# The start of a fused convolution and feed-forward kernel on one core: softmax, bands, masks and exchanges arranged differently

## The chip, the cores and the metric

The kernel runs on one core of a Trainium2 chip. The core has TensorE (matrix products, called PE in the profile, its weight loads PEld), VectorE (DVE), ScalarE (ACT), GpSimd (POOL) and SyncE (SP). Each takes its own instructions in order, and they wait for each other by semaphores. The metric is the device time of one execution in microseconds (us). Times in the text are us from the start of the profiled span.

## The reference

What is computed is a lightweight convolution followed by a multiplicative feed-forward layer.

```python
# x: (8, 3904, 192), weight: (8 heads, 7 taps)
w = softmax(weight, axis=-1)
out[b, s, h*24:(h+1)*24] = sum over k of w[h, k] * x_padded[b, s + k, h*24:(h+1)*24]   # 6 zero rows ahead
t = out.reshape(31232, 192)
a = t @ w1          # 192 x 1024
b = t @ w2          # 192 x 1024
h = (a * b) @ w3    # 1024 x 1024
result = h @ w_out  # 1024 x 192, float32
```

Since nothing stands between `w3` and `w_out`, the kernel multiplies these two with each other once (`W_sb`) and then uses their product.

## The kernel before, in words

The tokens are cut into two halves (`NS = 2`), which are worked side by side: half r sits on partitions 64r to 64r + 63, so that two products with 64 rows each run in TensorE at once. The convolution works on windows of 64 rows, of which 58 are new tokens. For each head it is a product with a band matrix, `Aband`, that holds the seven softmax weights on seven diagonals. The windows go in blocks; their number in each block stands in `SIZES` (line 50), and there are 270 in all.

**The prologue** (lines 132 to 213). ScalarE's queue loads the 8 x 7 weights into all 128 partitions (line 133), and GpSimd's queue loads x for block 0 (lines 98 and 129). GpSimd then makes `cmask`, seven diagonals of 64 x 64 (line 148), and starts the loads of `w1` and `w2`, with the identity for transposes between their halves (lines 159 to 166). TensorE meanwhile multiplies zeros 16 times (`warm`, lines 169 to 174). VectorE and ScalarE compute the softmax in every partition (lines 180 to 188). `band(g, copies)` (line 201) makes the bands of four heads: a product of masks and weights (`cprod`, line 203), three adds (line 211), and two copies that exchange the partition halves (line 213). It is called once per half of the heads; the first half's convolution stands between.

**The first block.** `conv(b, h0, nh)` (line 229) does 16 products for four heads into one PSUM tile, `cps`, and copies it into `convo` in pieces (line 255). `pe_transposes(b)` (line 287) turns `convo` by TensorE and copies the result into three tiles `xT` (line 300): the first and third on VectorE, the second on ScalarE. `swap_w(k, half, engines)` (line 315) makes `wsw`, a copy of the weights `wn` with the partition halves exchanged, 64 x 512 at a time (line 318). There are twelve such copies, six for each half of the columns.

**The rounds.** `first_product(R)` (line 326) does 512 tokens of each half. For each of eight column tiles ft, twelve products fill two PSUM tiles `pa` and `pb` (line 339); ScalarE copies `pa` into `asb` (line 345), and VectorE multiplies it with `pb` into `abT` (line 346). PSUM has four such tiles (`banks`), given out in turn, and conv, transposes, `warm` and the rounds all draw on them. `second_product` (line 351) multiplies `abT` with `W_sb`. The order of all work is written out by hand: a dictionary names what follows each ft in rounds 0 to 2 (conv of the next blocks, their transposes, and `fold`, which makes `W_sb`). From round 3 on, `xT` is filled by DMA transposes from `rows` in HBM.

**The queues.** GpSimd issues all loads of x, `w1`, `w2`, `w3` and `w_out` in program order between its own instructions, and after eight of them waits for an older one to land before it issues the next. The main part calls, in this order: load x of blocks 1 and 2, band, conv, band, three more `warm`, an exchange, conv, transposes, the other exchanges, and the later loads (lines 404 to 424).

Of the kernel before, what the change touches and what calls it, by code (L numbers as in the profile page):

```python
# [8 lines left out]

FP32 = mybir.dt.float32  # L10
# [7 lines left out]
def kernel(  # L18
# [53 lines left out]
    def slot(shape, dtype, name):  # L72
        return stage.tile(shape, dtype, tag="slot", bufs=5, name=name)
# [55 lines left out]
            nc.gpsimd.dma_start(out=xb[Q * r + PAD:Q * r + Q, 0, :],  # L129
                                in_=x_rows[r * TS:r * TS + ST, :])  # L130
# [8 lines left out]
    zeros = const.tile([128, CH], BF16)  # L139
    nc.vector.memset(zeros, 0.0)  # L140
    nc.scalar.activation(out=tiny, in_=tiny, func=ACT.Exp)

    ones = const.tile([128, 1], BF16)
    nc.gpsimd.memset(ones, 1.0)
    cmask = const.tile([128, K, Q], BF16)
    for r in range(NS):
        ps = slice(Q * r, Q * r + Q)
        nc.gpsimd.affine_select(
            out=cmask[ps], in_=ones[ps].unsqueeze(2).to_broadcast([Q, K, Q]),
            pattern=[[-1, K], [-1, Q]], compare_op=ALU.is_equal,  # L150
            fill=0.0, base=0, channel_multiplier=1)
    wn = [const.tile([128, DFF], BF16, name=f"wn{k}", tag=f"wn{k}") for k in range(3)]
    wsw = [const.tile([128, DFF], BF16, name=f"ws{k}", tag=f"ws{k}") for k in range(3)]

# [7 lines left out]
        nc.gpsimd.dma_start(out=wn[1][:, cs], in_=moe_w2[0:128, cs])  # L162

    load_w(0)
    ident = const.tile([128, 128], BF16)
    make_identity(nc, ident)
    load_w(1)

    def warm(n):
        t = banks("warm")  # L170
        for j in range(n):
            nc.tensor.matmul(t[:, j % 2, :], zeros[:, 0:128], zeros, start=True, stop=True)  # L172

    warm(16)


    wmax = const.tile([128, H], FP32)
    wsum = const.tile([128, H], FP32)
    wsb = const.tile([128, 2, 2, K], BF16)
    nc.vector.reduce_max(out=wmax, in_=wall, axis=AX.X)  # L180
    nc.vector.tensor_tensor(
        out=wall, in0=wall, in1=wmax.unsqueeze(2).to_broadcast([128, H, K]), op=ALU.subtract)
    nc.scalar.activation(out=wall, in_=wall, func=ACT.Exp)
    nc.vector.reduce_sum(out=wsum, in_=wall, axis=AX.X)
    nc.vector.reciprocal(out=wsum, in_=wsum)
    for r in range(NS):
        ps = slice(Q * r, Q * r + Q)
        nc.vector.tensor_tensor(
            out=wsb[ps],
            in0=wall[ps].rearrange("p (g a e) k -> p g a e k", g=2, a=2)[:, :, r],  # L190
            in1=wsum[ps].rearrange("p (g a e) -> p g a e", g=2, a=2)[:, :, r].unsqueeze(3)
                .to_broadcast([Q, 2, 2, K]),
            op=ALU.mult)

    Aband = const.tile([128, 2, 2, 2, Q], BF16)

# [1 line left out]
        g, j, e = h // 4, (h % 4) // 2, h % 2  # L198
        return Aband[Q * r:Q * r + Q, g, int(j != r), e, :]

    def band(g, copies):
        c = slot([128, 2, K, Q], BF16, "cprod")
        nc.vector.tensor_tensor(  # L203
            out=c,
            in0=cmask.unsqueeze(1).to_broadcast([128, 2, K, Q]),
            in1=wsb[:, g].unsqueeze(3).to_broadcast([128, 2, K, Q]),
            op=ALU.mult)
        for out, i0, i1 in ((c[:, :, 0:3], c[:, :, 0:3], c[:, :, 4:7]),
                            (c[:, :, 0:2], c[:, :, 0:2], c[:, :, 2:4]),
                            (Aband[:, g, 0], c[:, :, 0], c[:, :, 1])):  # L210
            nc.vector.tensor_tensor(out=out, in0=i0, in1=i1, op=ALU.add)  # L211
        for f, d, e in zip(copies, (Q, 0), (0, Q)):
            f(out=Aband[d:d + Q, g, 1], in_=Aband[e:e + Q, g, 0])


    xT = [const.tile([128, RING], BF16, name=f"xT{k}", tag=f"xT{k}") for k in range(NP)]
# [12 lines left out]
    def conv(b, h0, nh, evict=None):  # L229
        n = SIZES[b] // 2  # L230
        if h0 == 0:
            convo_of[b] = work.tile([128, n, NP, NS, Q], BF16, tag="convo", bufs=2, name="convo")
        convo = convo_of[b]
        cps = banks("cps")
        wd = nh * G

        def view(ps, r):
            return cps[ps, r, 0:n * wd].rearrange("p (w g) -> p w g", g=wd)

        for j in range(nh):  # L240
            h = h0 + j
            for c in range(2):
                xb, w0 = xb_of[b][c]
                for r in range(NS):
                    nc.tensor.matmul(  # L245
                        view(slice(Q * c, Q * c + Q), r)[:, :, j * G:(j + 1) * G],
                        band_of(h, r),
                        xb[Q * r:Q * r + Q, w0:w0 + n, h * G:(h + 1) * G],
                        start=True, stop=True)
        src = cps[:, :, 0:n * wd].rearrange("p r (w g) -> p r w g", g=wd)  # L250
        o = 0
        for e, (k, c0, m) in enumerate(segments(h0 * G, wd)):
            dst = convo[:, :, k, :, c0:c0 + m].rearrange("p w r g -> p r w g")
            f = evict or [nc.scalar.copy]
            f[e % len(f)](out=dst, in_=src[:, :, :, o:o + m])  # L255
            o += m
        if h0 + nh == H:
            del xb_of[b]
# [25 lines left out]
                    nc.sync.dma_start(out=dst[s0:s1], in_=src[s0:s1])  # L284
                w += m

    def pe_transposes(b):
        n = SIZES[b] // 2
        convo = convo_of[b]
        tps = banks_bf16("tps")  # L290
        for k in range(NP):
            for w in range(n):
                nc.tensor.transpose(
                    out=tps[:, k * n + w, :],
                    in_=convo[:, w, k].rearrange("p r g -> p (r g)"), identity=ident)
        t0 = tok(FIRST[b])
        for k in range(NP):
            dst = xT[k][:, t0:t0 + 2 * n * ST].rearrange("p (c w s) -> p c w s", c=2, w=n)
            src = tps[:, k * n:(k + 1) * n, :].rearrange("p w (c s) -> p c w s", c=2)
            (nc.scalar.copy if k == 1 else nc.vector.tensor_copy)(out=dst, in_=src[:, :, :, 0:ST])  # L300

    def transposes(R, first=0):
        t0, t1 = max(R * CH, first), min((R + 1) * CH, TS)
# [73 lines left out]
    def load_wo():  # L377
        nc.gpsimd.dma_start(out=wo_b, in_=wor)
# [34 lines left out]
    swap_w(2, 0, (V, A))  # L413
    swap_w(1, 0, (V, A))
    for k in (0, 2, 1):
        swap_w(k, 1, (P, A))
    load_wo()
    for jt in range(4):
        load_w3(jt)
    load_x(3)  # L420
    for jt in range(4, JT):
        load_w3(jt)
    for b in (4, 5, 6):
        load_x(b)

    def seq(*fs):
        def run():
            for f, *a in fs:
                f(*a)
        return run  # L430

    def fold(jt):
        if jt < JT:
            w3_transpose(jt)
        if jt > 0:
            w3_product(jt - 1)

    first_product(0, {
        2: seq((conv, 1, 0, 4)),
        4: seq((conv, 1, 4, 4)),  # L440
        6: seq((pe_transposes, 1)),
        7: seq((conv, 2, 0, 4))})
    first_product(1, {
# [90 lines left out]
```

## Time and profile before

| | us |
|---|---|
| median of the runs shown | 537.17 |
| lowest and highest of the three | 536.29 and 537.28 |
| the profiled execution's own time | 537.5 |
| its span, first to last instruction | 535.4 |
| TensorE busy within the span | 524.8 |
| VectorE busy | 349.7 |
| ScalarE busy | 326.3 |
| GpSimd busy | 49.1 |

The span is what the profile covers; the profiled execution's own time is longer by what lies around it. A TensorE that is busy is not one at its peak, since its products are pipelined and their ends are modelled. A row of a timeline has the start, the length, the engine, the line, the operation, the tile written and the tiles read, their sizes, and in brackets how long the engine had been idle and what ended that.

### The profile page before, as it was taken

How to read it: one execution, taken by the hardware profiler on the slowest of the kernel's cores; microseconds unless marked ns; L12 is line 12 of the kernel's file. 1: busy time of each engine (PE TensorE's matmuls, PEld its weight loads, DVE VectorE, ACT ScalarE, POOL GpSimd, SP SyncE). 2: the span in 40 equal slices, each digit the busy share in tenths (PEclk: the TensorE clock that was granted, in tenths of full speed). 3: DMA queues.
4: the chain of work that ended last, by engine and by line, in shares of the span. 5: the costliest groups of instructions: out<-in, count | busy, mean ns of one | idle time of the engine just before them, and what ended most of it. 6: DMA issues, size and time to landing. Idle time of an engine off the chain costs nothing.

```text
span 535.4 us, 12799 instructions
## 1 busy us (share of the span) xinstructions
PE 524.8 (98%) x5504; PEld 346.7 (65%) x5504; DVE 349.7 (65%) x329; ACT 326.3 (61%) x373; POOL 49.1 (9%) x87
## 2 busy tenths in 40 slices
PE   7999999999999999999999999999999999999996
PEld 2455584765858567585675857658576684856676
DVE  5577729669395784948849397593966929377470
ACT  3866647557474665747647475573756747475562
POOL 8641001001010010200101000020000000000000
PEclk9899999999999999999999999999999999999999
DMA  8999466766389555995569736593307443130304
GB/s 100 184 203 192 76 149 146 121 177 74 124 154 148 121 67 144 135 145 118 68 164 146 145 88 97 148 143 116 77 31 187 83 133 78 61 103 12 110 1 149
DMA packets 130587, 63.13 MB, mean 118 GB/s; under 512 B 83398, under 2 KB 129506, under 8 KB 130530
## 3 DMA queue, kind: packets, MB, share of 16 engines
q1 hardware_dynamic: 91842, 45.65, 36.4%
q0 software_dynamic: 38544, 16.63, 26.7%
q8 instruction: 43, 0.70, 0.6%
q14 instruction: 14, 0.11, 0.1%
q10 hardware_dynamic: 144, 0.03, 0.0%
HBM read 33.28 MB, written 34.82 MB: 127 GB/s over the span
## 4 chain that ended last, share of the span: by engine, by line
PE 92%; DVE 3%; ACT 2%; DMA 1%; issue 1%; ACTq 0%; DVEq 0%
PE ops L357 31%; PE pa L339 29%; PE pb L339 28%; PE cps L245 3%; DVE abT L346 2%; ACT asb L345 1%; PE wps L397 1%; PE w3ps L388 1%; DMA wall<-in_weight_dram 1%; ACT ws L318 1%; DVE cprod L203 0%; DVE cprod L211 0%; DVE xT L300 0%; ACT convo L255 0%; ACT xT L300 0%
## 5 line engine op out<-in xcount | busy, mean ns | idle before, releaser
L346 DVE TENSOR_TENSOR abT<-asb,pb 128x1024 bf16<-128x1024 bf16 (+1 forms) x248 | 298.1, 1204 | 56.3 <-ACT asb L345 41.0
L345 ACT CAST asb<-pa 128x1024 bf16<-128x1024 f32 (+1 forms) x248 | 247.6, 999 | 69.8 <-PE pa L339 69.0
L339 PE MATMUL pb<-xT,wn 64*128 64x512 bf16 (+1 forms) x744 | 202.2, 373 | 0.4
L339 PE MATMUL pa<-xT,wn 64*128 64x512 bf16 (+1 forms) x744 | 199.1, 374 | 1.7 <-DVE xT L300 1.1
L339 PE MATMUL pa<-xT,ws 64*128 64x512 bf16 (+1 forms) x744 | 199.2, 374 | 0.1
L339 PE MATMUL pb<-xT,ws 64*128 64x512 bf16 (+1 forms) x744 | 194.6, 374 | 0.0
L339 PEld LDWEIGHTS <-wn 64*128 64x128 bf16 x1488 | 137.8, 94 | 81.1 <-issue 5.6
L339 PEld LDWEIGHTS <-ws 64*128 64x128 bf16 x1488 | 128.3, 94 | 70.9 <-issue 5.6
L357 PE MATMUL ops<-W_sb,abT 128*128 128x192 bf16 x1952 | 166.3, 246 | 0.0
L357 PEld LDWEIGHTS <-abT 128*128 128x128 bf16 x1952 | 159.6, 98 | 9.9 <-issue 9.5
L362 ACT COPY osb<-ops 128x768 f32<-128x768 f32 (+1 forms) x62 | 48.9, 788 | 117.0 <-PE ops L357 117.0
L255 DVE CAST convo<-cps 128x864 bf16<-128x864 f32 (+10 forms) x46 | 37.9, 858 | 104.3 <-PE cps L245 101.2
L108 POOL DMA_DIRECT2D xb<-in_x_dram x36 | 28.6, 804 | 13.6 <-PE pa L339 4.6
L487 POOL COPY pace<-abT 1x2 bf16<-1x2 bf16 x9 | 1.6, 174 | 270.3 <-DVE abT L346 270.3
L255 ACT CAST convo<-cps 128x640 bf16<-128x640 f32 (+9 forms) x40 | 22.6, 607 | 1.1 <-PE cps L245 0.6
L245 PE MATMUL cps<-xb,Aband 64*64 64x432 bf16 (+3 forms) x384 | 18.8, 285 | 1.9 <-DVE Aband L211 1.4
L245 PEld LDWEIGHTS <-Aband 64*64 64x64 bf16 x384 | 7.1, 105 | 10.8 <-issue 7.7
L172 PE MATMUL warm<-zeros 128*128 128x512 bf16 x19 | 7.3, 559 | 1.4 <-DVE zeros L140 1.4
L397 PE MATMUL wps<-wo_b,w3T 128*128 128x192 bf16 x64 | 6.6, 246 | 0.4 <-DVE xT L300 0.4
L399 ACT CAST W_sb<-wps 128x192 bf16<-128x192 f32 x8 | 2.5, 319 | 5.9 <-PE wps L397 5.9
L388 PEld LDWEIGHTS <-w3b 128*128 128x128 bf16 x64 | 3.7, 98 | 3.4 <-issue 3.4
L172 PEld LDWEIGHTS <-zeros 128*128 128x128 bf16 x19 | 2.4, 135 | 5.4 <-issue 3.8
(46 smaller groups left out, 58.9 us busy)
## 6 DMA issues: line engine op xcount, KB each, us to landing
out_dram<-osb SPq DMA_DIRECT2D x60, 384.0 KB
xb<-in_x_dram POOLq DMA_DIRECT2D x18, 432.0 KB, 7.0
rows<-convo SPq DMA_DIRECT2D x8, 648.0 KB
w3b<-in_moe_w_dram POOLq DMA_DIRECT2D x8, 256.0 KB, 10.9
xb<-in_x_dram POOLq DMA_DIRECT2D x4, 384.0 KB, 12.4
xb<-in_x_dram POOLq DMA_DIRECT2D x4, 336.0 KB, 10.0
xT<-rows SPq DMA_TRANSPOSE x84
rows<-convo SPq DMA_DIRECT2D x4, 288.0 KB
```

Of the source, the lines that this page charges most:

```text
L108: nc.gpsimd.dma_start(out=xb[Q * r:Q * r + Q, w:w + m, :], in_=x_spans(r, i, m))
L172: nc.tensor.matmul(t[:, j % 2, :], zeros[:, 0:128], zeros, start=True, stop=True)
L245: nc.tensor.matmul(view(slice(Q * c, Q * c + Q), r)[:, :, j * G:(j + 1) * G], band_of(h, r), xb[Q * r:Q * r + Q, w0:w0 + n, h * G:(h + 1) ...
L255: f[e % len(f)](out=dst, in_=src[:, :, :, o:o + m])
L318: f(out=wsw[k][d:d + Q, cs], in_=wn[k][e:e + Q, cs])
L339: nc.tensor.matmul(p[:, r, 0:N], w_of(i, k, r)[rs, ft * 128:(ft + 1) * 128], xT[k][rs, r0:r0 + N], start=(k == 0), stop=(k == NP - 1))
L345: nc.scalar.copy(out=asb[:, :, 0:N], in_=pa[:, :, 0:N])
L346: nc.vector.tensor_tensor(out=ab[:, ft, :, 0:N], in0=asb[:, :, 0:N], in1=pb[:, :, 0:N], op=ALU.mult)
L357: nc.tensor.matmul(ops[:, g // 2, (g % 2) * D:(g % 2) * D + D], ab[:, jt, r, g * 128:(g + 1) * 128], W_sb[:, jt, :], start=(jt == 0), stop ...
L362: nc.scalar.copy(out=osb.rearrange("p (a g) d -> p a (g d)", g=2), in_=ops[:, 0:ng // 2, 0:2 * D])
L388: nc.tensor.transpose(out=tps[:, gt, :], in_=w3b[:, gt * 128:(gt + 1) * 128], identity=ident)
L397: nc.tensor.matmul(wps[:, 0, 0:D], w3T[:, gt, :], wo_b[:, gt, :], start=(gt == 0), stop=(gt == JT - 1))
```

## The change

- **Softmax.** The weights are loaded once, with a head per partition (8 x 7). The sum comes with the exponential, as its accumulated output. A product with a diagonal puts the weights of head h into row h alone, and one matmul with ones spreads them over 128 partitions into PSUM. Two copies on VectorE bring them into `wsb`, each weight twice side by side.
- **Masks.** GpSimd makes one diagonal, `diag`, 70 columns wide, ahead of the loads of x. VectorE copies seven blocks of it into `cmask` and two into the identity.
- **Bands.** One product and three adds make the bands of all eight heads, and two copies exchange the halves, one on ScalarE and one on VectorE.
- **Warm.** Five and seven products of zeros, around the spreading matmul, take the place of 16 and three.
- **First block.** Both convs follow each other; each is copied out of PSUM by both engines.
- **Exchanges.** ScalarE did six, VectorE three and GpSimd three. Now VectorE does six, ScalarE three and GpSimd three, and some of them stand in round 0 behind ft 1 and ft 2.
- **Order.** The x of block 2 and all later loads are issued behind GpSimd's exchanges. Block 1 has 8 windows and block 3 has 18. The two convs of block 1 stand behind ft 4 and 5 of round 0.

```diff
-    SIZES = [10, 10, 10, 16, 16, 20] + [36] * 5 + [10]
+    SIZES = [10, 8, 10, 18, 16, 20] + [36] * 5 + [10]
...
-    wall = const.tile([128, H, K], FP32)
-    nc.scalar.dma_start(out=wall, in_=weight.partition_broadcast(128))
-    load_x(0)
-    load_first()
+    taps = const.tile([H, K], FP32)
+    nc.scalar.dma_start(out=taps, in_=weight)
+    diag = const.tile([128, Q + K - 1], BF16)
+    nc.gpsimd.memset(diag, 1.0)
     for r in range(NS):
         ps = slice(Q * r, Q * r + Q)
         nc.gpsimd.affine_select(
-            out=cmask[ps], in_=ones[ps].unsqueeze(2).to_broadcast([Q, K, Q]),
-            pattern=[[-1, K], [-1, Q]], compare_op=ALU.is_equal,
+            out=diag[ps], in_=diag[ps], pattern=[[-1, Q + K - 1]], compare_op=ALU.is_equal,
             fill=0.0, base=0, channel_multiplier=1)
+    load_x(0)
+    load_first()
...
+    for k in range(K):
+        nc.vector.tensor_copy(out=cmask[:, k], in_=diag[:, k:k + Q])
+    for r in range(NS):
+        ps = slice(Q * r, Q * r + Q)
+        nc.vector.tensor_copy(out=ident[ps, ps], in_=diag[ps, 0:Q])
...
-    warm(16)
...
+    warm(5)
+    nc.vector.reduce_max(out=low, in_=taps, axis=AX.X, negate=True)
+    nc.scalar.activation(out=taps, in_=taps, func=ACT.Exp, bias=low, accum_out=total)
+    nc.vector.reciprocal(out=total, in_=total)
+    nc.vector.scalar_tensor_tensor(
+        out=share, in0=taps.unsqueeze(1).to_broadcast([H, H, K]), scalar=total,
+        in1=diag[0:H, 0:H].unsqueeze(2).to_broadcast([H, H, K]), op0=ALU.mult, op1=ALU.mult)
+    spread = banks("spread")
+    nc.tensor.matmul(spread[:, 0, 0:H * K], one_rows, share.rearrange("h a k -> h (a k)"),
+                     start=True, stop=True)
+    wsb = const.tile([128, 2, 2, K, 2], BF16)
     for r in range(NS):
         ps = slice(Q * r, Q * r + Q)
+        nc.vector.tensor_copy(
             out=wsb[ps],
+            in_=spread[ps, 0, 0:H * K].rearrange("p (g a e k) -> p g a e k", g=2, a=2, e=2)
+                [:, :, r].unsqueeze(4).to_broadcast([Q, 2, 2, K, 2]))
+    warm(7)
...
+    nc.vector.tensor_tensor(
+        out=cprod.rearrange("p h k (s two) -> p h k s two", two=2),
+        in0=cmask.rearrange("p k (s two) -> p k s two", two=2).unsqueeze(1)
+            .to_broadcast([128, 4, K, Q // 2, 2]),
+        in1=wsb.rearrange("p g e k two -> p (g e) k two").unsqueeze(3)
+            .to_broadcast([128, 4, K, Q // 2, 2]),
+        op=ALU.mult)
...
+    nc.scalar.copy(out=Aband[Q:128, :, 1], in_=Aband[0:Q, :, 0])
+    nc.vector.tensor_copy(out=Aband[0:Q, :, 1], in_=Aband[Q:128, :, 0])
...
-    for b in (1, 2):
-        load_x(b)
-    band(0, (A, A))
-    conv(0, 0, 4)
-    band(1, (V, A))
-    warm(3)
-    swap_w(0, 0, (V, A))
+    load_x(1)
+    conv(0, 0, 4, evict=(A, V))
     conv(0, 4, 4, evict=(V, A))
-    pe_transposes(0)
-    swap_w(2, 0, (V, A))
-    swap_w(1, 0, (V, A))
-    for k in (0, 2, 1):
-        swap_w(k, 1, (P, A))
-    load_wo()
...
+    pe_transposes(0, lambda: swap_w(0, 0, (V, V)))
+    swap_w(2, 0, (A, V))
+    swap_w(1, 0, (A, V))
+    swap_w(0, 1, (P, P))
...
+    def later_loads():
+        swap_w(1, 1, (P, V))
+        load_x(2)
+        load_wo()
...
     first_product(0, {
-        2: seq((conv, 1, 0, 4)),
-        4: seq((conv, 1, 4, 4)),
+        1: seq((swap_w, 2, 1, (V, A))),
+        2: later_loads,
+        4: seq((conv, 1, 0, 4)),
+        5: seq((conv, 1, 4, 4)),
```

The second argument of `pe_transposes` is called behind the first of the three copies out of PSUM.

More of the change, by code (lines that the diff above doesn't have):

```diff
@@ L6 @@
 from concourse import bass_utils, mybir
-from concourse.masks import make_identity
 from concourse._compat import with_exitstack
@@ L172, in warm @@
             nc.tensor.matmul(t[:, j % 2, :], zeros[:, 0:128], zeros, start=True, stop=True)
-    warm(16)
[L177 to L185, printed above, removed]
+    warm(5)
+    low = const.tile([H, 1], FP32)
+    total = const.tile([H, 1], FP32)
+    share = const.tile([H, H, K], BF16)
+    nc.vector.reduce_max(out=low, in_=taps, axis=AX.X, negate=True)
[8 more added lines that the diff above has]
+    wsb = const.tile([128, 2, 2, K, 2], BF16)
     for r in range(NS):
         ps = slice(Q * r, Q * r + Q)
-        nc.vector.tensor_tensor(
+        nc.vector.tensor_copy(
             out=wsb[ps],
[L190 to L193, printed above, removed]
+            in_=spread[ps, 0, 0:H * K].rearrange("p (g a e k) -> p g a e k", g=2, a=2, e=2)
+                [:, :, r].unsqueeze(4).to_broadcast([Q, 2, 2, K, 2]))
+    warm(7)
     Aband = const.tile([128, 2, 2, 2, Q], BF16)
@@ L199, in band_of @@
         return Aband[Q * r:Q * r + Q, g, int(j != r), e, :]
[L201 to L213, printed above, removed]
+    cprod = stage.tile([128, 4, K, Q], BF16, tag="cprod", bufs=1, name="cprod")
+    nc.vector.tensor_tensor(
[5 more added lines that the diff above has]
+        op=ALU.mult)
+    for o, i0, i1 in ((cprod[:, :, 0:3], cprod[:, :, 0:3], cprod[:, :, 4:7]),
+                      (cprod[:, :, 0:2], cprod[:, :, 0:2], cprod[:, :, 2:4])):
+        nc.vector.tensor_tensor(out=o, in0=i0, in1=i1, op=ALU.add)
+    pairs = cprod.rearrange("p (g e) k s -> p g e k s", g=2)
+    nc.vector.tensor_tensor(out=Aband[:, :, 0], in0=pairs[:, :, :, 0], in1=pairs[:, :, :, 1],
+                            op=ALU.add)
+    nc.scalar.copy(out=Aband[Q:128, :, 1], in_=Aband[0:Q, :, 0])
+    nc.vector.tensor_copy(out=Aband[0:Q, :, 1], in_=Aband[Q:128, :, 0])
     xT = [const.tile([128, RING], BF16, name=f"xT{k}", tag=f"xT{k}") for k in range(NP)]
```

34 lines of the change are left out of this document (18 added, 16 removed).

## The prediction

> **What bounds the kernel now.** First I read the page's chain that ended last, then the table of stages, then the chain in order of time up to 45 us, and then each engine's timeline for the first 18 us. All times are from the span's start.
>
> ```profile
> span 535.4 us, 12799 instructions
> ...
> PE 92%; DVE 3%; ACT 2%; DMA 1%; issue 1%; ACTq 0%; DVEq 0%
> ```
> ```profile
> 14.00:60.00 46.00, 44.09 (x480) 23.43 (x481) 31.73 (x36) 33.18 (x48) 16.54 (x26) 0.96 1.29 172
> 60.00:100.00 40.00, 40.00 (x444) 25.67 (x442) 26.73 (x25) 26.09 (x31) 1.86 (x3) 1.00 0.71 138
> ```
> ```profile
> 24.94 0.65 PE pb L339 x6
> ...
> 30.53 1.23 DVE abT L346
> ```
>
> TensorE carries 92% of the chain, and its busy time (the first figure behind the length of the stage) fills 60 to 100 us entirely. Before that it does not: between 14 and 60 us it is idle 1.9 us. Up to round 0's last product (30.53 + 1.23 = 31.75) the chain goes by VectorE and ScalarE. So the change, which touches the start and round 0, is worth what it moves that 31.75: after it the order of work is the same and TensorE has nothing to wait with.
>
> The start itself, by engine (start, length, releaser in brackets); VectorE:
>
> ```profile
> 4.72 0.21 DVE L180 TENSOR_REDUCE wmax<-wall 128x8 f32<-128x56 f32 x1 [3.39 <-DMA wall<-in_weight_dram]
> 4.97 0.58 DVE L181 TENSOR_TENSOR wall<-wall,wmax 128x56 f32<-128x56 f32 x1
> ...
> 6.34 0.38 DVE L188 TENSOR_TENSOR wsb<-wall,wsum 64x28 bf16<-64x28 f32 x2
> 6.83 1.09 DVE L203 TENSOR_TENSOR cprod<-cmask,wsb 128x896 bf16<-128x896 bf16 x1
> 7.96 0.68 DVE L211 TENSOR_TENSOR cprod<-cprod 128x384 bf16<-128x384 bf16 x2
> 8.67 0.22 DVE L211 TENSOR_TENSOR Aband<-cprod 128x128 bf16<-128x128 bf16 x1
> ...
> 10.91 0.43 DVE L213 COPY Aband<-Aband 64x128 bf16<-64x128 bf16 x1
> 11.37 0.29 DVE L318 COPY ws<-wn 64x512 bf16<-64x512 bf16 x1
> 11.85 0.49 DVE L255 CAST convo<-cps 128x320 bf16<-128x320 f32 x1 [0.18 <-PE cps L245]
> 13.61 0.46 DVE L300 COPY xT<-tps 128x580 bf16<-128x580 bf16 x1 [1.27 <-PE tps L293]
> ```
> ScalarE:
> ```profile
> 5.58 0.25 ACT L183 ACTIVATE wall<-wall 128x56 f32<-128x56 f32 x1 [2.86 <-DVE wall L181]
> ...
> 12.37 0.69 ACT L255 CAST convo<-cps 128x640 bf16<-128x640 f32 x1 [0.52 <-DVE convo L255]
> 14.10 0.64 ACT L300 COPY xT<-tps 128x580 bf16<-128x580 bf16 x1 [1.04 <-DVE xT L300]
> 14.77 2.69 ACT L318 COPY ws<-wn 64x512 bf16<-64x512 bf16 x5
> 17.49 1.01 ACT L345 CAST asb<-pa 128x1024 bf16<-128x1024 f32 x1
> ```
> TensorE and its clock (the column before the last two):
> ```profile
> 1.39 6.45 PE L172 MATMUL warm<-zeros 128*128 128x512 bf16 x16 [1.39 <-DVE zeros L140]
> ...
> 11.40 0.40 PE L245 MATMUL cps<-xb,Aband 64*64 64x120 bf16 x15 [0.23 <-DVE Aband L213]
> ...
> 13.12 0.45 PE L293 MATMUL tps<-ident,convo 128*128 128x128 bf16 x5 [0.27 <-ACT convo L255]
> ```
> ```profile
> 13.00:14.00 1.00, 0.45 (x5) 0.37 (x6) 0.39 (x1) 0.06 (x1) 0.96 (x2) 0.99 1.23 144
> 14.00:17.00 3.00, 2.81 (x13) 1.06 (x14) 0.93 (x4) 2.87 (x6) 3.00 (x6) 0.50 1.27 141
> 17.00:18.00 1.00, 1.00 (x10) 0.74 (x8) 0.00 (x0) 0.98 (x2) 1.00 (x3) 0.80 1.59 189
> ```
> GpSimd, and how long the DMAs of x take to land:
> ```profile
> 1.32 1.67 POOL L98 DMA_DIRECT2D xb<-in_x_dram  x2 [0.80 <-POOLq L518]
> 2.97 1.09 POOL L129 DMA_DIRECT2D xb<-in_x_dram  x2
> 4.02 0.14 POOL L144 MEMSET ones<- 128x1 bf16 x1
> 4.24 1.25 POOL L148 TENSOR_SCALAR_AFFINE_SELECT cmask<-ones 64x448 bf16<-64x448 bf16 x2
> ```
> ```profile
> xb<-in_x_dram POOLq DMA_DIRECT2D x2, 216.0 KB, 4.7
> xb<-in_x_dram POOLq DMA_DIRECT2D x2, 21.8 KB, 4.1
> ```
>
> The reader should see one chain: weight landed (4.72), softmax, two bands (to 11.34), conv, evictions, transposes, xT (14.07), and then five exchanges on ScalarE (2.69) which keep round 0's first asb until 17.49.
>
> **The change part by part.**
>
> *Masks.* They now stand ahead of x on GpSimd: a memset (0.14) and two selects 70 wide. The 448 wide ones took 0.62 each; a narrow one lies between 0.1 and that; I take 0.45, so 1.05 in all, and the diagonal is ready near 2.2 if GpSimd can begin near 1.0 (its first row now stands at 1.32, VectorE begins at 0.91). Then VectorE cuts nine blocks of 64 out of it. No row has such a copy: 0.43 (the 64x128 exchange at 10.91) is the upper end, a good 0.1 the lower, since eight times the width takes 0.29 (11.37). I take 0.13: done near 3.4. The weights, 224 bytes instead of 28 KB, land between 1.2 (end of issue) and 4.7; I take 3.3. So the reduce starts near 3.5, not 4.72. GpSimd loses its wide selects and ident, so the weight loads come no later than now.
>
> *Softmax.* Before, 4.72 to 6.83: 2.11. After: reduce 0.2, exp 0.25, reciprocal as much as a reduce, 0.2, the masked product 0.2, a matmul of 56 columns 0.3 (five transposes take 0.45), two copies 0.4, and six handovers of 0.03: 1.7. The subtraction of 0.58 is gone. The band product starts near 5.2.
>
> *Bands.* The product has 1792 elements. At the rate of the old one (0.93 of its 1.09 for 896) it takes 2.0; at that of the adds (0.68 for 384 and 256, 0.22 for 128: 0.55 to 0.6 ns an element) it takes 1.1. I take 1.1, since both inputs now run in pairs of neighbours as in the adds. [...] Adds of 768, 512 and 256 by the slope: 0.57 + 0.43 + 0.29 = 1.3. With handovers 7.7; the exchange of 256 on both engines (0.43 for 128 on VectorE, 0.54 for 512 on ScalarE, 2.69/5) about 0.45: bands complete at **8.15, against 11.34**.
>
> *x.* Its last DMA was issued at about 3.5 and landed by 7.1 to 7.6; conv started at 8.95, so 1.3 us of cover. Moved 0.9 later, it lands at 8.0 to 8.5. Cover is gone, and conv starts at **8.2 to 8.3** with either.
>
> *Conv to xT.* Before, the first conv's evictions lay beside the second band, and 11.40 to 14.07 was 2.7. Now all four evictions stand in a row (ScalarE, VectorE, VectorE, ScalarE, since an eviction waits for the other engine's on the same tile, as at 12.37): 0.70 + 0.50 + 0.50 + 0.70 and gaps, 2.5. Ahead of it conv 0.4, behind it transposes 0.47 and xT 0.47, or 0.6 and 0.73 at half clock. xT is ready at 12.05, or **12.5** at half clock. So 1.6 to 2.0 is left of the 3.2.
>
> *The clock.* Before, 16 warm matmuls took 6.45 without a gap. The clock was full up to 14.0, then 0.50, and full again from 17.4 (0.80 in the slice to 18). After, five and seven matmuls at 0.40 (6.45/16) are bursts of 2.0 and 2.8 with a gap of over 1 us, so I count on half clock until 17.4 again, for conv, transposes and the first products.
>
> *Exchanges.* ScalarE keeps two of its five (1.08) ahead of asb, VectorE gets four (0.25 to 0.29 each), GpSimd three, in time for ft 4 near 20. At half clock pairs of matmuls take 0.43 (0.65/3 at full): ws0 at 13.0, xT2 at 13.6, ws2 at 13.9, so pa is done at 14.5 and **asb starts at 14.5, not 17.49**; pb at 15.7, abT at 15.8. Half clock costs 2.6 per ft instead of 1.3, so asb 1 starts at 17.1 (before, 18.5 at the earliest, behind asb 0) and abT 1 at 18.1. From here full speed: asb 2 has an exchange of 0.55 ahead of it on ScalarE, abT 2 and abT 3 one of 0.28 each on VectorE: they start at 19.7 and 21.2. Conv 1 follows at ft 4 and 5 (before 2 and 4), which only swaps the order; its evictions of 0.9, the transposes' three copies one after the other, and asb and abT bring the last abT to 29.4 to **30.6, against 31.75**. The same bookkeeping for before gives 31.95, so the gain is 1.1 to 1.3.
>
> *The rest.* Sizes 8 and 18 instead of 10 and 16 keep the windows' number. The x of block 2 goes behind three exchanges on GpSimd (1.8), which leaves it landing near 18 (4.7 behind an issue near 13), and it is needed at ft 7, near 26. VectorE's three further exchanges (0.8) lie in round 0 and are in the sum.
>
> **Sum.** 1.3 us off the profiled execution's 537.5 (span 535.4 and 2.1 around it) is 536.2. The median, 537.17, lies 0.33 below that execution: **535.9**.
>
> **The rivals.**
>
> *Full clock.* If the second burst is enough, or the clock isn't lowered before the products, xT is at 12.05, asb at 13.8, and each ft takes 1.3 at once: the last abT ends at 28.9 and the time is about 534.2. For it: the clock was still 0.99 from 13 to 14, when TensorE had long had short bursts only (busy 0.45). Against it: 16 matmuls in one burst had gone ahead of that, and the clock fell at 14.0 all the same. [...]
>
> *Late bands.* The product at 2.0, or copies and selects at their upper ends, put conv at 9 to 10. A us there costs only 0.6 to 0.8 at round 0's end, since half-speed matmuls wait for the clock either way: 536.2 to 537.2. With that goes the case that the change does its work and the gain is lost later.
>
> *Slower.* VectorE's nine copies wait for GpSimd's writing of DMA descriptors, which now begins just then. For it: the subtraction at 4.97 took 0.58 and ended with GpSimd's selects (5.49), and the 64x128 copy at 10.91 took more than a 64x512 one. Against it: the products and adds from 6.34 to 8.9 ran beside such DMAs unharmed. Held through x's four DMAs (2.76), conv starts near 10.8 and nothing is won; it turns slower by more than 0.2% once conv starts after about 11.9. Held through the first four weights as well (2.3 more), conv starts near 12.5, round 0 ends 1.5 later, and the time is 538.7.
>
> **How the numbers follow.** Forecast 0.55 (own range 535.3 to 536.5), full clock 0.18, late bands or gain lost 0.12, slower 0.15. A measurement of this kernel can tell about 0.2% (1.07 us) from no change, so the forecast falls 0.39 to faster and 0.16 to the same: faster 0.57, same 0.28, slower 0.15. The range leaves out the slower case and reaches beyond full clock by its 0.3: 533.9 to 538.0.
>
> **What would show it.** Right: reduce near 3.5, band product of 1.1 near 5.2, conv near 8.2, xT near 12.5, asb near 14.5, round 0's last abT ending near 30.6, TensorE's clock 0.50 up to 17 or so. Wrong: copies of the diagonal over 0.3 each, a product of 2.0, x as releaser of conv well after 8.5, clock 1.00 at 14 us, or a round 0 that ends after 31.7 in spite of an early asb.

## The result and the profile after

The changed kernel takes 535.84 us (median of 20 runs, 534.86 to 536.97), the kernel before 537.12 (20 runs beside them, 536.29 to 537.87). The ratio is 0.9974, with a 95% interval from 0.9966 to 0.9981: 1.28 us are won. The profiled execution after took 535.81.

The page of the kernel after, its span and the chain that ended last:

```profile
span 534.1 us, 12779 instructions
...
PE 93%; DVE 2%; ACT 2%; DMA 1%; issue 1%; POOL 0%; ACTq 0%; POOLq 0%
```

VectorE's timeline of the kernel after (start, length, line, tiles, idle time before and what ended it):

```profile
1.60 0.87 DVE L155 COPY cmask<-diag 128x64 bf16<-128x64 bf16 x7
2.21 0.47 DVE L158 COPY ident<-diag 64x64 bf16<-64x64 bf16 x2
2.72 0.15 DVE L185 TENSOR_REDUCE low<-taps 8x1 f32<-8x7 f32 x1
...
4.54 1.09 DVE L210 TENSOR_TENSOR cprod<-cmask,wsb 128x1792 bf16<-128x1792 bf16 x1
5.67 1.02 DVE L219 TENSOR_TENSOR cprod<-cprod 128x768 bf16<-128x768 bf16 x2
6.72 0.29 DVE L221 TENSOR_TENSOR Aband<-cprod 128x256 bf16<-128x256 bf16 x1
7.04 0.22 DVE L224 COPY Aband<-Aband 64x256 bf16<-64x256 bf16 x1
8.97 0.89 DVE L266 CAST convo<-cps 128x320 bf16<-128x320 f32 x2 [1.71 <-ACT convo L266]
11.39 0.46 DVE L311 COPY xT<-tps 128x580 bf16<-128x580 bf16 x1 [1.53 <-PE tps L304]
11.77 1.30 DVE L331 COPY ws<-wn 64x512 bf16<-64x512 bf16 x2
...
15.98 1.22 DVE L359 TENSOR_TENSOR abT<-asb,pb 128x1024 bf16<-128x1024 bf16 x1 [1.89 <-PE pb L352]
17.78 1.22 DVE L359 TENSOR_TENSOR abT<-asb,pb 128x1024 bf16<-128x1024 bf16 x1 [0.58 <-ACT asb L358]
...
28.98 1.22 DVE L359 TENSOR_TENSOR abT<-asb,pb 128x1024 bf16<-128x1024 bf16 x1 [0.52 <-ACT asb L358]
```

ScalarE's timeline of the kernel after:

```profile
2.90 0.30 ACT L186 ACTIVATE taps<-taps,low 8x7 f32<-8x7 f32 x1
3.10 0.18 ACT L186 ACTIVATION_READ_ACCUMULATOR taps<-taps,low 8x1 f32 x1
7.04 0.40 ACT L223 COPY Aband<-Aband 64x256 bf16<-64x256 bf16 x1 [3.75 <-DVE Aband L221]
8.24 0.69 ACT L266 CAST convo<-cps 128x640 bf16<-128x640 f32 x1 [0.80 <-PE cps L256]
9.89 0.69 ACT L266 CAST convo<-cps 128x640 bf16<-128x640 f32 x1 [0.95 <-DVE convo L266]
11.88 0.64 ACT L311 COPY xT<-tps 128x580 bf16<-128x580 bf16 x1 [1.30 <-DVE xT L311]
12.55 1.13 ACT L331 COPY ws<-wn 64x512 bf16<-64x512 bf16 x2
14.62 1.01 ACT L358 CAST asb<-pa 128x1024 bf16<-128x1024 f32 x1 [0.93 <-PE pa L352]
16.73 1.01 ACT L358 CAST asb<-pa 128x1024 bf16<-128x1024 f32 x1 [1.10 <-PE pa L352]
```

GpSimd's timeline of the kernel after:

```profile
1.05 0.53 POOL L138 TENSOR_SCALAR_AFFINE_SELECT diag<-diag 64x70 bf16<-64x70 bf16 x2
1.52 1.71 POOL L97 DMA_DIRECT2D xb<-in_x_dram  x2
...
11.67 1.99 POOL L331 COPY ws<-wn 64x512 bf16<-64x512 bf16 x3 [1.15 <-DMA wn<-in_moe_w_dram]
```

TensorE's timeline of the kernel after:

```profile
1.27 2.31 PE L178 MATMUL warm<-zeros 128*128 128x512 bf16 x5 [1.27 <-DVE zeros L142]
...
3.96 2.61 PE L178 MATMUL warm<-zeros 128*128 128x512 bf16 x7
7.59 0.82 PE L256 MATMUL cps<-xb,Aband 64*64 64x120 bf16 x32 [1.02 <-DMA xb<-in_x_dram]
```

The table of stages of the kernel after (length; TensorE's busy time first behind it; the granted clock is the third column from the end). The cuts are 3.41 us apart, for a reason that comes out below:

```profile
2.46:5.87 3.41, 3.17 (x9) 0.98 (x8) 2.50 (x10) 0.82 (x4) 3.41 (x8) 1.00 1.00 110
5.87:9.28 3.41, 1.81 (x40) 0.97 (x38) 1.60 (x5) 1.09 (x2) 2.91 (x7) 1.00 1.11 143
9.00:10.00 1.00, 0.56 (x7) 0.36 (x8) 0.86 (x2) 0.11 (x1) 1.00 (x3) 0.64 0.99 137
10.00:16.00 6.00, 4.80 (x25) 2.00 (x27) 2.64 (x7) 3.37 (x5) 4.68 (x8) 0.50 0.99 122
16.00:17.00 1.00, 1.00 (x12) 0.51 (x10) 1.00 (x1) 0.27 (x1) 1.00 (x3) 0.94 1.35 161
```

The gain shrinks on its way. The bands are complete at 7.44 (7.04 + 0.40) instead of 11.34: 3.9 earlier. The first part of `xT` is written (11.39 + 0.46) at 11.85 instead of 14.07: 2.2 earlier. Round 0's last `abT` ends at 30.20 (28.98 + 1.22) instead of 31.75: 1.55 earlier. The median is 1.28 lower.

Behind round 0 little differs. The profiled execution's own time less the end of round 0's last `abT` is 505.75 before and 505.61 after, and lies between 505.3 and 505.9 in all fourteen kernels of the table below. So the question is what sets that end. Two things are suspects. The four evictions of the first two convs stand in a row from 8.24 to 10.58, each but the first waiting for the one ahead of it; and the clock is 0.50 from 10 to 16.

### The profile page after: what moved, and what is told of

It is laid out like the page before. It is cut to its first block, busy times and chain, and to the rows that moved or that the text cites. A ratio compares the mean times of both kernels' runs of the same rounds, so it can differ in the third digit from the quotient of the medians.

```text
span 534.1 us, 12779 instructions
## 1 busy us (share of the span) xinstructions
PE 523.2 (98%) x5495; PEld 345.9 (65%) x5495; DVE 350.5 (66%) x339; ACT 324.0 (61%) x368; POOL 47.9 (9%) x85
## 4 chain that ended last, share of the span: by engine, by line
PE 93%; DVE 2%; ACT 2%; DMA 1%; issue 1%; POOL 0%; ACTq 0%; POOLq 0%
PE ops L370 31%; PE pa L352 29%; PE pb L352 29%; PE cps L256 3%; DVE abT L359 2%; ACT asb L358 2%; PE wps L410 1%; DMA xb<-in_x_dram 1%; PE w3ps L401 1%; POOL xb L97 0%; DVE ws L331 0%; PE tps L304 0%; ACT convo L266 0%; DVE xT L311 0%; DVE convo L266 0%
## 5 line engine op out<-in xcount | busy, mean ns | idle before, releaser
L266 ACT CAST convo<-cps 128x864 bf16<-128x864 f32 (+9 forms) x39 | 22.3, 611 | 2.3 <-PE cps L256 1.4
L256 PE MATMUL cps<-xb,Aband 64*64 64x432 bf16 (+5 forms) x384 | 18.1, 285 | 1.3 <-DMA xb<-in_x_dram 1.0
L178 PE MATMUL warm<-zeros 128*128 128x512 bf16 x12 | 4.9, 576 | 1.3 <-DVE zeros L142 1.3
L410 PEld LDWEIGHTS <-w3T 128*128 128x128 bf16 x64 | 5.2, 98 | 0.9 <-issue 0.5
```

The lines of the kernel that those rows point to most:

```text
L256: nc.tensor.matmul(view(slice(Q * c, Q * c + Q), r)[:, :, j * G:(j + 1) * G], band_of(h, r), xb[Q * r:Q * r + Q, w0:w0 + n, h * G:(h + 1) ...
L410: nc.tensor.matmul(wps[:, 0, 0:D], w3T[:, gt, :], wo_b[:, gt, :], start=(gt == 0), stop=(gt == JT - 1))
```

## The experiments

All are edits of the kernel after, except the sixth. The ratio is to the kernel before, run on the same chip: its median beside e1 to e4 was 537.12, beside e5 to e8 537.54 and beside e9 to e12 537.40, so 0.4 us between rows of different groups says little. "Clock" is the mean granted clock of each run over its span; that of before is from the 23 runs beside e1 to e4. A run that is at half clock for 6.8 us of 534 shows 0.994 (the profiled execution of after), one with half as long 0.997 (that of before); half speed from the start on is not counted in it (e8_nowarm shows that).

| kernel | median us (runs) | ratio, 95% interval | clock of the runs | round 0's last abT ends |
|---|---|---|---|---|
| before | 537.12 (20) | | 0.990 to 1.000 | 31.75 |
| after | 535.84 (20) | 0.9974 [0.9966, 0.9981] | 0.990 to 0.997 | 30.20 |
| e1_fill | 534.11 (6) | 0.9942 [0.9927, 0.9958] | 0.998 to 1.000 | 28.54 |
| e2_evict | 533.02 (6) | 0.9930 [0.9912, 0.9949] | 1.000 in four, 0.995 in two | 27.35 |
| e3_single | 536.56 (12) | 0.9987 [0.9977, 0.9997] | 0.989 to 0.994 | 31.20 |
| e4_oldswap | 535.81 (12) | 0.9975 [0.9963, 0.9987] | 0.992 to 0.997 | 29.36 |
| e5_both | 534.19 (6) | 0.9942 [0.9929, 0.9954] | 0.999 to 1.000 | 28.63 |
| e6_before_fill | 537.37 (12) | 0.9995 [0.9982, 1.0008] | 0.996 to 1.000 | 32.31 |
| e7_pool | 535.74 (5) | 0.9968 [0.9956, 0.9980] | 0.992 to 0.997 | 30.15 |
| e8_nowarm | 536.12 (7) | 0.9977 [0.9966, 0.9988] | 0.998 to 1.000 | 30.59 |
| e9_evict_oldswap | 534.28 (6) | 0.9943 [0.9928, 0.9958] | 0.995 to 1.000 | 28.59 |
| e10_evict_fill2 | 533.20 (6) | 0.9925 [0.9910, 0.9940] | 0.998 to 1.000 | 27.79 |
| e11_evict_pool | 533.46 (6) | 0.9937 [0.9916, 0.9958] | 0.990 to 1.000 | 27.58 |
| e12_oldorder | 534.97 (7) | 0.9960 [0.9947, 0.9974] | 0.993 to 0.997 | 30.53 |

My theory was that the half clock and the row of evictions eat the gain; the rivals were that the exchanges of weights, or the order of round 0, do.

**e1_fill: keep TensorE busy between the evictions.**

```diff
-    def warm(n):
-        t = banks("warm")
+    def warm(n, t=None):
+        t = banks("warm") if t is None else t
...
-    warm(7)
+    filler = warm(7)
...
     conv(0, 4, 4, evict=(V, A))
-    pe_transposes(0, lambda: swap_w(0, 0, (V, V)))
+    warm(3, filler)
+    pe_transposes(0, lambda: swap_w(0, 0, (V, V)), (2, 2, 4))
```

The new last argument of `pe_transposes` is the number of zeros behind each third of the transposes.

> The changed kernel, with products of zeros put into TensorE's idle time between conv and the first round (3, then 2, 2 and 4). Nothing else differs. Theory (round 0's end decides, and TensorE's half clock until about 16 us is a part of it): the clock stays at 1.00 from about 6 us on, the first asb starts near 13.8 instead of 14.62, round 0's last abT ends near 29.2 instead of 30.2, and the time is 0.6 to 1.2 us below the changed kernel's 535.84 (near 535.0). Rival (ScalarE and VectorE bound round 0, and the clock is hidden behind them): round 0 ends within 0.3 us of 30.2, and the time stays at 535.8.

Two rows of its table of stages:

```profile
9.00:10.00 1.00, 0.91 (x10) 0.47 (x9) 0.56 (x2) 0.40 (x1) 1.00 (x2) 1.00 0.92 128
...
14.00:16.00 2.00, 2.00 (x22) 0.88 (x19) 1.22 (x1) 1.29 (x3) 2.00 (x3) 1.00 0.58 56
```

TensorE does 22 matmuls in the two us from 14, where e8 below does 8 in one at half speed. The first `asb` starts at 13.27 instead of 14.62; some 0.3 of that is x, which landed earlier in this execution (conv starts at 7.07 instead of 7.59, the first eviction at 7.95 instead of 8.24). The time is 534.11: 1.7 below after, more than the 0.6 to 1.2 expected, with the evictions as they were. The zeros cost little where TensorE would wait (the first product starts at 11.60, 0.3 behind `xT`), and in six runs of six the clock stays up.

**e2_evict: one engine per conv.**

```diff
-    conv(0, 0, 4, evict=(A, V))
-    conv(0, 4, 4, evict=(V, A))
+    conv(0, 0, 4, evict=(A, A))
+    conv(0, 4, 4, evict=(V, V))
```

> The changed kernel, with the first conv copied out by ScalarE alone and the second by VectorE alone, so that the four pieces do not wait for each other in a row. Theory (the row of evictions gave back about 0.8 us of what the bands won): the last eviction ends near 9.8 instead of 10.58, xT is ready near 11.1 instead of 11.85, and round 0 ends 0.3 to 0.7 earlier; time near 535.3. Rival (xT is not what the first products wait for, the exchange of the weights is): xT earlier, but the first asb within 0.2 us of 14.62 and the time the same.

ScalarE's timeline, then VectorE's:

```profile
8.04 1.02 ACT L266 CAST convo<-cps 128x640 bf16<-128x640 f32 x2 [0.50 <-PE cps L256]
10.51 0.64 ACT L311 COPY xT<-tps 128x580 bf16<-128x580 bf16 x1 [1.45 <-DVE xT L311]
11.18 1.33 ACT L331 COPY ws<-wn 64x512 bf16<-64x512 bf16 x2
12.45 1.01 ACT L358 CAST asb<-pa 128x1024 bf16<-128x1024 f32 x1
```
```profile
8.25 1.22 DVE L266 CAST convo<-cps 128x320 bf16<-128x320 f32 x2 [0.89 <-PE cps L256]
...
26.13 1.22 DVE L359 TENSOR_TENSOR abT<-asb,pb 128x1024 bf16<-128x1024 bf16 x1 [0.51 <-ACT asb L358]
```

ScalarE's pair (1.02) and VectorE's (1.22) now lie side by side and end at 9.47, not 10.58. The first `asb` starts at 12.45, 2.2 earlier than after. That is more than the evictions' 1.1: in four runs of six the clock stayed full as well. Those take 532.83 to 533.06; the two with 0.995 take 534.31 and 534.72, where after takes 535.02 (median of its nine runs at 0.995 and 0.997). From these two runs I estimate that the evictions alone are worth some 0.5 and the clock the rest; no run separates them.

**e3_single: each weight once.** The band product reads one weight 64 times over, as before the change, instead of pairs.

```diff
-    wsb = const.tile([128, 2, 2, K, 2], BF16)
+    wsb = const.tile([128, 2, 2, K], BF16)
...
-        out=cprod.rearrange("p h k (s two) -> p h k s two", two=2),
-        in0=cmask.rearrange("p k (s two) -> p k s two", two=2).unsqueeze(1)
-            .to_broadcast([128, 4, K, Q // 2, 2]),
+        out=cprod,
+        in0=cmask.unsqueeze(1).to_broadcast([128, 4, K, Q]),
-        in1=wsb.rearrange("p g e k two -> p (g e) k two").unsqueeze(3)
-            .to_broadcast([128, 4, K, Q // 2, 2]),
+        in1=wsb.rearrange("p g e k -> p (g e) k").unsqueeze(3).to_broadcast([128, 4, K, Q]),
```

> The changed kernel with each weight stored once, so that the band product reads one element again and again, as the kernel before did. Theory (pairs of neighbours are what halves the product): the product takes 2.0 us instead of 1.09, the bands are complete near 8.4 instead of 7.44, conv starts 0.9 later than 7.6, and the time rises by 0.4 to 0.8 us, to about 536.4. Rival (the bands have slack behind x's landing or the weights' exchange): the product takes 2.0, and the time rises by less than 0.2 us. Second rival (the pairs don't matter for the rate): the product still takes 1.1.

```profile
4.51 2.03 DVE L210 TENSOR_TENSOR cprod<-cmask,wsb 128x1792 bf16<-128x1792 bf16 x1
```

2.03 instead of 1.09. Doubling the weights costs 0.06 in two copies (0.44 against 0.38) and saves 0.94 at once. The forecast had the two rates from the rows of before: 1.1 for pairs from the adds, 2.0 for one weight read again and again from the old product. Round 0 ends 1.0 later and the median rises by 0.7: by the medians a us at the bands is worth about 0.75 at the end.

**e4_oldswap: the old exchanges,** six on ScalarE ahead of the first `asb`, three on VectorE, three on GpSimd.

```diff
-    pe_transposes(0, lambda: swap_w(0, 0, (V, V)))
-    swap_w(2, 0, (A, V))
-    swap_w(1, 0, (A, V))
-    swap_w(0, 1, (P, P))
+    pe_transposes(0)
+    for k in (0, 2, 1):
+        swap_w(k, 0, (V, A))
+    for k in (0, 2, 1):
+        swap_w(k, 1, (P, A))
...
-        swap_w(1, 1, (P, V))
...
-        1: seq((swap_w, 2, 1, (V, A))),
```

> The changed kernel with the exchanges of the weights as before: each first-half copy shared by VectorE and ScalarE behind the transposes, each second-half copy by GpSimd and ScalarE, and none in round 0. Theory (xT and the half clock set the first products, the exchanges only partly): ScalarE's six copies of 0.54 run from 12.5 to about 15.8, the first asb starts near 15.8 instead of 14.62, round 0's end comes 0.3 to 0.7 later (VectorE is spared three copies), time near 536.3. Rival (the exchanges are the gain): round 0 ends near 31.7 as in the kernel before and the time is 537.

```profile
12.07 3.21 ACT L331 COPY ws<-wn 64x512 bf16<-64x512 bf16 x6
15.31 1.95 ACT L358 CAST asb<-pa 128x1024 bf16<-128x1024 f32 x2
```

The first `asb` is held until 15.31 and the time does not move: 535.81, and at equal clock too (at 0.997, 535.22 and 535.24 against a median of 535.0 after). The second follows at once (1.95 for both), where after has its second at 16.73. At half clock TensorE keeps the second `asb` of after until 16.73 anyway, so ScalarE has time for its exchanges; this reason is argued, since the execution profiled here was at half clock for 3.4 us only, and after's for 6.8. **The part of the change that its title names last is worth nothing that these runs can tell in this kernel.**

**e5_both:** e1 and e2 together.

> The changed kernel with the zeros in TensorE's idle time and with each conv copied out by one engine. Theory (two costs, a row of evictions of 0.8 us that counts whole, and a clock that depends on TensorE's activity in a window whose phase is chance): the clock is 0.998 or more in every run, where the evictions alone had 0.995 in two of six, and every run lies at 532.7 to 533.3, like the full-clock runs of the evictions alone (532.92). Rival (the zeros delay the transposes): 0.3 to 0.6 above 532.92 in spite of the clock.

TensorE's timeline:

```profile
10.13 0.44 PE L305 MATMUL tps<-ident,convo 128*128 128x128 bf16 x5
10.40 1.03 PE L178 MATMUL warm<-zeros 128*128 128x512 bf16 x4
11.37 0.39 PE L355 MATMUL pa<-xT,wn 64*128 64x512 bf16 x1
```

534.19, worse than e2 and than the rival had it, though every run has a clock of 0.999 or more. With the evictions early, the zeros are no longer in a gap: they stand ahead of ready work. Those between the transposes put the first `xT` at 10.61 (10.02 in e2), and the four behind the last transposes keep the first product until 11.37 (10.53 in e2), 0.3 behind `xT`.

**e6_before_fill: zeros in the kernel before,** one behind its second conv and (1, 1, 3) in its transposes.

```diff
-    warm(3)
+    filler = warm(3)
...
-    pe_transposes(0)
+    warm(1, filler)
+    pe_transposes(0, (1, 1, 3))
```

> The kernel before with zeros in TensorE's idle time behind its second conv (1, then 1, 1 and 3), nothing else. Theory (the clock is worth about 0.8 us to the kernel before as well, since its runs at 1.00 have 536.33 and those at 0.997 have 537.12): clock 0.998 or more in every run and about 536.3; the changed kernel with zeros (534.11) is then 2.2 better at equal clock. Rival (the clock only goes along with something else that makes these runs fast): clock 1.00, but the time stays at 537.1.

537.37, no difference that can be told. The zeros moved the first `xT` from 13.61 to 14.17 and the clock fell early all the same (0.50 from 10 to 12). Its six runs at 0.998 or more take 535.86 to 537.09, its six at 0.996 and 0.997 take 537.64 to 538.51, so the clock goes along with 2 us here; the four at 0.997 take 538.3 to 538.5, where before takes 537.12. So an equal mean clock doesn't make an equal time, and the run doesn't separate the clock from the delay.

**e7_pool: GpSimd's exchanges later,** with block 2's x ahead of them.

```diff
+    load_x(2)
     swap_w(0, 1, (P, P))
...
-        load_x(2)
```

> The changed kernel with x of block 2 loaded ahead of GpSimd's three exchanges instead of behind them, so that these start about 1.5 us later and not beside VectorE's two. Theory (VectorE's copies wait while GpSimd copies, which is why two took 1.30 instead of 0.58): the two take 0.6, the second product of round 0 starts 0.6 earlier, and since TensorE is at half clock there the end is 0.2 to 0.4 earlier, 535.5. Rival (something else lengthened the two, as their weights' landing): they still take over 1 us.

```profile
11.29 0.58 DVE L331 COPY ws<-wn 64x512 bf16<-64x512 bf16 x2
```

VectorE's pair takes 0.58 instead of 1.30, and the time stays: 535.74 against 535.84. After, the pair ran beside GpSimd's copies (11.67 to 13.66); here GpSimd is idle from 11 to 12. That the longer pair cost time is not shown.

**e8_nowarm:** all twelve zeros are left out (they enter no result).

```diff
-    warm(5)
...
-    warm(7)
```

> The changed kernel without the five and seven products of zeros. Theory (they bring full clock for conv in some runs, but never up to the first round): clock share 0.988 to 0.992 in all runs, conv and transposes at half clock take 0.4 to 0.6 us more, time 0.4 to 0.8 above 535.84. Rival (twelve products of zeros no longer do anything for the clock): the time is within 0.2 of 535.84.

Two rows of its table of stages:

```profile
14.00:15.00 1.00, 1.00 (x8) 0.35 (x6) 0.00 (x0) 0.67 (x1) 1.00 (x2) 1.00 0.48 56
...
18.00:19.00 1.00, 1.00 (x12) 0.42 (x10) 1.00 (x1) 0.98 (x2) 1.00 (x3) 1.00 1.59 190
```

536.12, 0.3 above after, which is less than the intervals can tell: in the kernel after the zeros buy nearly nothing. In the profile after, the clock that they bring is gone by 9.28. A warning for the reader: the clock column says 1.00 in both rows, but 8 matmuls in a us against 12 say that TensorE was at half speed in the first. In this run the column shows 1.00 from the start, though the products start 0.40 to 0.43 apart up to 16.64 and 0.21 to 0.22 from there on, and conv's 32 took 1.25 (after's 0.82); the matmuls' count is the safer witness.

**e9_evict_oldswap:** e2 with the exchanges of e4.

> The changed kernel with each conv copied out by one engine, and with the exchanges of the weights as in the kernel before. Theory (the exchanges were worth nothing in the changed kernel because half-speed products hid ScalarE's copies; with xT earlier and TensorE at full clock they are in the way): ScalarE copies from 11.2 to 14.4, the first asb starts near 14.4 instead of 12.45, and the time is 0.8 to 1.6 us above the 533.02 of the evictions alone. Rival (the exchanges never matter, since VectorE is spared three copies): within 0.4 us of 533.02.

```profile
11.12 3.40 ACT L331 COPY ws<-wn 64x512 bf16<-64x512 bf16 x6
14.54 2.09 ACT L358 CAST asb<-pa 128x1024 bf16<-128x1024 f32 x2
```

534.28, 1.26 worse than e2. The execution profiled here was at half clock from 11.86 to 15.28, but the four runs at 1.000 take 534.16 to 534.42, where e2's four take 532.83 to 533.06: the same 1.3 at equal clock. So the new exchanges do matter once `xT` is early and the clock full: then ScalarE, not TensorE, is late (14.54 against 12.45).

**e10_evict_fill2:** e2 with `warm(2, filler)` behind the second conv and fill (0, 0, 2), fewer zeros than e5.

> The changed kernel with each conv copied out by one engine and only two products of zeros behind the second conv and two behind the transposes, where TensorE has nothing to do. Theory (the longer row of zeros lost 1.3 us by its own length, not by the clock): transposes and first products start as with the evictions alone, the clock is 0.998 or more in more runs than four of six, and the time is 532.8 to 533.1. Rival (zeros cost what they save): 533.3 or more.

533.20. All six runs have a clock of 0.998 or more, where two of e2's six fell to 0.995; six runs each are few to tell that apart. It lies 0.3 above e2's full-clock runs (532.92 in the median) and between theory and rival; whether the zeros cost that isn't shown, since VectorE's second pair of exchanges took 0.91 in this profile and 0.50 in e2's. The two are equal within their intervals, and both beat after by 2.6 to 2.8 and before by about 4 us.

**e11_evict_pool:** e2 with the order of e7.

> The changed kernel with each conv copied out by one engine and x of block 2 loaded ahead of GpSimd's exchanges. Theory (GpSimd's copies beside VectorE's are an accident of a few hundred ns, and with xT at 10.5 VectorE's are done before GpSimd begins): within 0.2 us of 533.02. Rival (the collision costs time in all these kernels): 0.3 or more below 533.02.

533.46, with one run of 536.31 at 0.990, and 532.88 to 533.24 in the three runs with a clock of 1.00: nothing is added to e2.

**e12_oldorder: conv 1 behind ft 2 and ft 4 again,** with the old block sizes.

```diff
-    SIZES = [10, 8, 10, 18, 16, 20] + [36] * 5 + [10]
+    SIZES = [10, 10, 10, 16, 16, 20] + [36] * 5 + [10]
...
-        2: later_loads,
-        4: seq((conv, 1, 0, 4)),
-        5: seq((conv, 1, 4, 4)),
+        2: seq((later_loads,), (conv, 1, 0, 4)),
+        4: seq((conv, 1, 4, 4)),
```

> The changed kernel with the old sizes of the blocks and the two convs of block 1 behind ft 2 and ft 4 again. Theory (the order within round 0 only moves the same work): round 0's last abT ends within 0.5 us of 30.2 and the time within 0.4 us of 535.84. Rival (the later place of block 1 is a part of the gain): 0.5 us or more above 535.84.

The median of 534.97 lies 0.9 below after, more than I expected. But three of its seven runs have a clock of 0.997 and take 534.76 to 534.97, where after takes 535.0 (median of eight such runs); its two at 0.993 take 535.94 and 536.08, after's one 536.07. At equal clock there is no difference of more than 0.3, so the order is hardly what moved the median.

## Why the prediction was right, point by point

The forecast was 535.9, by a round 0 that ends at 30.6; it was 535.84 and 30.20. The range held it. The mechanism was right (an earlier start, halved by half clock and evictions, worth 1.1 to 1.3 at round 0's end by the forecast, and 1.55 in the profiled runs), but three terms of the sum were off and partly cancelled. That the time agrees to 0.1 is luck: nine of the 20 runs after take 534.86 to 535.56, the other eleven 535.81 to 536.97, and the median lies at the edge between the two groups.

- **What bounds round 0: nearly right.** Up to 31.75 the chain of before goes by VectorE and ScalarE, but TensorE's products (L339) have 3.0 us of it, from 20.94 to 21.77 and from 24.12 to 26.25.
- **Masks and softmax: too slow in the forecast.** The two narrow selects took 0.53 together (I took 0.45 each, between the bounds of 0.1 and 0.62), the nine copies 1.08 (0.12 each; I took 0.13), and the weights had landed by 2.72. The forecast's own terms put the diagonal at 2.05, not at 2.2; it was ready at 1.58. So the reduce started at 2.72, not 3.5. The softmax took 1.82 against 1.7; ScalarE's read of its accumulated sum, 0.18 from 3.10, stands in it and wasn't counted.
- **Bands: right.** Product 1.09 (1.1, by the adds' rate; 2.03 without the pairs in e3), adds 1.02 + 0.29 (1.3). Complete at 7.44 instead of 8.15, by the reduce's earlier start.
- **x: mechanism right, size off.** x's first DMA was issued 0.2 later than before (1.52 against 1.32), not 0.9, and its last landing released conv at 7.59, not at 8.2. The cover is gone, as said: bands at 7.44 and x at 7.46 came together.
- **Row of evictions: right.** 8.24 to 10.58 is 2.34 (2.5 forecast), and e2 shows that the wait between engines is its cause.
- **The clock: half right.** I had half clock from conv to 17.4. In the profile after, the clock was full behind the second burst, and conv's 32 products took 0.82 (1.25 in e8, without the bursts). I had also read the column's 1.00 ahead of 14.0 in before as full clock, though the zeros' 0.40 each was half speed (the last section shows it). After the change it fell at about 9.28 and came back near 16.1, so only the transposes and the first products suffered. The full clock rival, which I priced at 534.2, is what e1 makes: 534.11.
- **Exchanges: wrong, without consequence.** VectorE's pair took 1.30 instead of 0.5, beside GpSimd's three copies, which ran from 11.67 to 13.66. It took back the 0.65 that the start had gained, and `asb` began at 14.62 (14.5 forecast), `abT` 0 at 15.98 (15.8), `asb` 1 at 16.73 (17.1), `abT` 1 at 17.78 (18.1). In e7, with GpSimd idle from 11 to 12, the pair took 0.58, and the half clock, which lasts until 17.66 there, holds `asb` 1 until 16.30 all the same.
- **What I credited wrongly.** I gave the exchanges a place in the sum as the reason why `asb` left 17.49. e4 puts them back and loses nothing that can be told: what the change wins here comes from the earlier start. Of the start's parts, only the doubled weights were taken back alone (e3); what masks, softmax and the joined bands are worth each is not shown.
- **The slower rival** didn't come. The nine copies took 1.08 in all, 0.12 each, the longest 0.42, beside GpSimd's DMA issues from 1.52 on; that an issue held any of them is not shown.

**Where the gain went.** Of 3.9 us at the bands, 1.7 were lost up to `xT` (x's landing, then the row of evictions and transposes at half clock), and another 0.65 in round 0, where half-speed products set the pace until 16.1. At equal clock the change is worth more than the medians say: of the runs with 0.997, four of the kernel before beside e1 to e4 take 537.12 in the median and eight of after 535.0, which is 2.1. But the kernel before had no half clock on record in 7 of its 23 runs there (536.33), and after had some in each of its 20 runs, and in 11 of them, at 0.994 or less, at least twice as long as at 0.997. That can account for the 0.8 between 2.1 and 1.28.

## What to carry to other kernels

A faster prologue pays only as far as the next thing is ready: here the input had 1.3 us of cover by the forecast's estimate, and PSUM tiles each copied out by two engines in turn ran as a chain (2.34 us for four copies, 1.43 in e2), so giving each engine a tile of its own was worth more (2.8 us with the clock) than the change itself (1.3). Count what keeps TensorE busy between short bursts before rearranging other engines' work; with products of zeros in a true gap the clock was 0.998 or more in six runs of six (e1; 0.990 to 0.997 after), and with the same zeros ahead of ready work the time was 1.2 us higher (e5 against e2). Compare runs at equal granted clock before believing a difference of one us, and remember that the mean leaves out half speed at the start and doesn't say where the half clock fell.

## What the runs showed of the hardware that I had not expected

**The stretches at half clock were 3.41 us long or twice that, and TensorE's busy time alone doesn't tell when they come.** In the profile after, the clock fell at about 9.28 (0.64 in the slice from 9 is 0.72 of it at half) and rose at about 16.12 (0.94 in the slice from 16), 6.84 apart; before, it fell at about 13.98 (0.99 from 13) and rose at 17.40 (0.80 from 17), 3.42 apart. Six more profiled executions have such a stretch at the start, worked out in the same way: 3.40 to 3.42 long in e4, e6 and e9, 6.82 in e3, e7 and e12. Steps of 3.41 us fit all eight, and one, two and three of them at half clock in a span of 534 us make 0.997, 0.994 and 0.990. Values between these can come from a second fall behind the last product, where it costs nothing: in e9 (0.995) TensorE is done at 528.26, and the clock falls again at 530.75. The kernel before, cut into such steps, and two steps of e4:

```profile
0.35:3.76 3.41, 2.37 (x6) 0.88 (x7) 0.42 (x3) 1.49 (x2) 2.61 (x8) 1.00 0.15 16
3.76:7.17 3.41, 3.41 (x9) 1.21 (x8) 1.90 (x7) 0.25 (x1) 3.29 (x8) 1.00 1.27 148
7.17:10.58 3.41, 2.19 (x22) 0.70 (x20) 3.24 (x7) 1.22 (x4) 3.29 (x8) 1.00 0.93 136
10.58:13.99 3.41, 2.00 (x32) 1.28 (x32) 1.86 (x6) 1.94 (x5) 3.37 (x6) 1.00 1.07 120
```
```profile
5.29:8.71 3.42, 1.83 (x37) 0.85 (x35) 1.92 (x5) 1.08 (x2) 3.20 (x7) 1.00 1.27 155
...
12.12:15.53 3.41, 2.79 (x14) 1.71 (x16) 1.64 (x4) 3.39 (x7) 3.15 (x5) 0.50 1.07 131
```

In before, the clock was still low behind a step with TensorE busy for 2.37 of 3.41: up to 6.91 the zeros' weight loads follow each other by 0.43 and only the last by 0.34, and the 16 zeros took 0.40 each where four at full clock took 1.03 in e5. In after, it was full behind a step with 3.17, with a gap of 0.24 in it: the second burst's weight loads follow each other by 0.43 up to 5.64, the last by 0.34. But over the eight executions the ranges overlap. The clock rose behind steps of 2.79 (e4) to 3.42 and stayed at half behind steps of 2.20 (after) to 2.86 (e7). It fell behind steps of 1.53 (e3) to 2.00 (before) and stayed full behind 1.83 (e4, whose groups of five transposes still took 0.45 in the step behind it, where five took 0.71 at half speed in e8), 1.99 (e9) and 2.19 (before). No step was idle when the clock fell (TensorE's longest gap in after's was 1.02). What else counts, no run settles; that TensorE's activity is judged over such a step, as the theory of e5 had it, is not shown either.

**Where the half clock begins, and how much of it there is, differs.** In the eight executions, each of another kernel, the first fall lies anywhere from 9.28 to 13.98, and no run shows what sets it. Of the 23 runs of the kernel before beside e1 to e4, those at 1.000 take 536.33 (7 runs, median), at 0.997 537.12 (4), at 0.994 537.59 (3) and at 0.990 538.4 (3), a spread larger than the change's gain; the other six have a clock in between, and one of them takes 537.11 at 0.999, which I can't explain.
